# V loads of a decode attention kernel issued by GpSimd instead of SyncE

## The chip, the cores and the metric

The kernel runs on one core of a Trainium2 chip. The time is device microseconds (us) of one execution; the kernel before takes 1980.17 us, the median of 3 runs (1979.96 to 1980.22).

## What is computed

Two attention blocks, A and B, of the same shape are computed one after the other, for a single new token (Sq = 1) against long caches. In each block there are 2 batches, 32 heads with a K and a V cache of 8192 x 192 bf16 each, x of 640 columns, a query weight wq (640 x 6144) and an output weight wo (6144 x 640):

```
q = x @ wq                      # split into 32 heads of 192
scores = q . k_cache * 192**-0.5
p = softmax(scores)             # over the 8192 positions
o = p . v_cache
out = concat_heads(o) @ wo      # A and B side by side in the output
```

Each K and each V of one head and batch is 3.146 MB (8192 x 192 x 2 bytes), and there are 128 of each, so 805 MB of caches are read once, and 31 MB of weights.

## The kernel before, in words

**Units.** The work is cut into NU = 128 units, numbered u: one head of one block for one batch. The two batches of a head follow each other; g = u // 2 counts heads over both blocks. A unit's K and V are laid out on 128 partitions, 64 positions a partition, so that each partition reads one contiguous row of 24,576 bytes from memory (`sp_k`, L198; `sp_v`, L207). K has NK = 2 buffers (`kb`), V has NV = 3 (`vb`).

**One unit.** VectorE multiplies K by the broadcast query, in two halves m0 and m1 (`dve_mul`, L230), into `prod`. TensorE adds `prod` up over groups of 16 columns by matmuls with an identity into PSUM (`pe_sum`, L295: 12 matmuls a half, signals s0 and s1); VectorE reduces what is left to 64 scores a partition (`dve_red`, L233, signals r0, r1), and takes their maximum (`dve_max`, L236). GpSimd makes it one maximum over all partitions (`pool_ar`, L220, signal ar), ScalarE scales it (L243) and takes the exponentials with their sums (`act_exp`, L246, signal exp), GpSimd adds the sums over partitions (`pool_ls`, L224, signal ls). TensorE then multiplies the probabilities with V, 32 matmuls (`pe_pv`, L306, signal pv). Every second unit ScalarE moves the result to SBUF (L253, L254); every fourth it is turned and normalised (f3, L314; f4, L260), and multiplied with wo (f5, L341). The queries of later heads are made by TensorE (L287) ahead of their use, from wq.

**Order on the engines.** Each engine has a list of operations by slot (`dve_tab`, `act_tab`, `pe_tab`, `pool_tab`); slot u is roughly unit u, and inside a slot the operations are sorted by a number. Each engine issues its list in order, and an operation that waits holds up all behind it. On TensorE slot u has the sums of unit u (number 0) and then pv of unit u - 1 (number 2); for the last two units the sums are moved up into slot 125 ahead of pv(124) (L369). On GpSimd slot u has ar(u) (number 0) and ls(u) (number 1).

**Order of the loads.** All cache and weight loads are issued by SyncE (SP), in the order built at L425 to L432 and emitted at L433 to L455: K(0), K(1), V(0), K(2), V(1) and so on, K(u) and then V(u-1), except that K(127) is put right behind K(126), ahead of V(125). K(u) waits for both multiplies of unit u - 2 (its buffer), V(u) for pv(u-3) (its buffer). wq of the next 8 heads and wo of the next 4 heads are put between. K(127) is loaded in two halves, V(126) in 2 parts and V(127) in 4 (VSPLIT, L141), each part with a semaphore of its own; the last two wo tiles follow at the end in a K buffer (L453). ScalarE issues the loads of x and half of the output.

**GpSimd's start.** Ahead of its slots GpSimd builds the identity, clears some tiles, and copies x of block B into its broadcast form (L457 to L467).

Of the kernel before, what the change touches and what calls it, by code (L numbers as in the profile page):

```python
# [51 lines left out]
def build_kernel(nc, blocks, out):  # L52
# [11 lines left out]
    NU = G * B  # L64
# [4 lines left out]
    NV = 3  # L69
# [12 lines left out]
    def unit(u):  # L82
        g = u // B
        return g // Hn, g % Hn, u % B, g
# [7 lines left out]
    with ExitStack() as es:  # L92
# [34 lines left out]
        S_sp = _Stream("sp", sem("s_sp"), reg)  # L127
# [13 lines left out]
        VSPLIT = {NU - 2: [0, T // 2, T], NU - 1: [0, T // 2, 3 * T // 4, 7 * T // 8, T]}  # L141
        vpsem = {(u, i): sem(f"vp{u}_{i}") for u, c in VSPLIT.items() for i in range(len(c) - 1)}

        def key(name, *idx):
            for i in idx:
                if i < 0:
                    return None
            return (name,) + tuple(idx)
# [21 lines left out]
        def dma(out_ap, in_ap, s):  # L170
            return lambda eng: eng.dma_start(out_ap, in_ap).then_inc(s, 16)  # L171
# [4 lines left out]
        def sp_wq(w):  # L176
            blk = (w * HQ) // Hn
            h0 = (w * HQ) % Hn
            src = blocks[blk]["wq"].rearrange("(j c) n -> j c n", c=DC)[:, :, h0 * Dh:(h0 + HQ) * Dh]
            return dma(wqs[:], src, wqsem)  # L180
# [10 lines left out]
        def sp_wo(w):  # L191
            blk = (w * HO) // Hn
            h0 = (w * HO) % Hn
            src = blocks[blk]["wo"][h0 * Dh:(h0 + HO) * Dh, :].rearrange("(pr p i) n -> p pr (i n)", p=128, i=3)
            i = w - (NWO - NLATE)
            return dma(wo_tile(w).rearrange("p pr i n -> p pr (i n)"), src, wosem[w % 2] if i < 0 else wlsem[i])

        def sp_k(u, part=None):  # L198
            blk, h, b, g = unit(u)
            src = blocks[blk]["k"][b, h].rearrange("(p t) d -> p t d", p=128)  # L200
            if part is None:
                return dma(kb[u % NK][:], src, ksem[u % NK])
            if part == 0:
                return dma(kb[u % NK][:, 0:TH, :], src[:, 0:TH, :], ksem[u % NK])
            return dma(kb[u % NK][:, TH:T, :], src[:, TH:T, :], k2sem[u])

        def sp_v(u, t0=0, t1=T, sm=None):  # L207
            blk, h, b, g = unit(u)
            src = blocks[blk]["v"][b, h].rearrange("(p t) d -> p t d", p=128)
            return dma(vb[u % NV][:, t0:t1, :], src[:, t0:t1, :], vsem[u % NV] if sm is None else sm)  # L210

        def vcuts(u):
            c = VSPLIT[u]
            return list(zip(c[:-1], c[1:]))
# [23 lines left out]
        def dve_f2(g):  # L238
            s0 = 64 * (g % 2)
            return lambda eng: eng.reciprocal(rcT[(g // 2) % 2][s0:s0 + 64, :], lall[g % 2][s0:s0 + 64, :])  # L240
# [8 lines left out]
        def act_f1(g, b0, b1):  # L249
            hs = g % 2  # L250

            def fn(eng):
                eng.activation(o_sb[0:1, b0:b1, hs, :], ops[hs][0:1, b0:b1, 0:Dh], ACTF.Identity)  # L253
                return eng.activation(o_sb[32:33, b0:b1, hs, :], ops[hs][32:33, b0:b1, Dh:2 * Dh], ACTF.Identity)  # L254
            return fn
# [22 lines left out]
        def pe_q(qg):  # L278
            pr, b = qg // 2, qg % 2
            g0 = 2 * pr  # L280
            blk = g0 // Hn
            w = g0 // HQ
            off = (g0 % HQ) * Dh

            def fn(eng):
                for c in range(DC):
                    ins = eng.matmul(qps[:, 0:QW], xbc[blk][b][:, c, :], wqs[:, c, off:off + QW],  # L287
                                     start=(c == 0), stop=(c == DC - 1))
                return ins
            return fn, [("wq", w), ("xbc", blk), key("a0", qg - 1)]  # L290
# [61 lines left out]
        pool_tab = [[] for _ in range(NSLOT)]  # L352

        def put(tab, slot, order, fn, waits, sig):
            tab[slot].append((order, len(tab[slot]), fn, waits, sig))

        for u in range(NU):
# [17 lines left out]
            else:  # L375
                cuts = vcuts(u)
                for i, (t0, t1) in enumerate(cuts):
                    put(pe_tab, u + 1, 2, pe_pv(u, t0 // 2, t1 // 2), (w0 if i == 0 else []) + [("vp", u, i)],
                        ("pv", u) if i == len(cuts) - 1 else None)

        for g in range(G):
            u1 = 2 * g + 1
            pp = g // 2
            w1 = [key("f3", pp - 1), ("init",)]
            if g == G - 1:
                put(act_tab, u1, 2, act_f1(g, 0, 1), [("pv", u1 - 1)] + w1, ("f1a", g))
                put(act_tab, u1 + 1, 2, act_f1(g, 1, 2), [("pv", u1), ("f1a", g)], ("f1", g))
            else:
                put(act_tab, u1 + 1, 2, act_f1(g, 0, 2), [("pv", u1)] + w1, ("f1", g))
            put(dve_tab, u1 + 1, 8, dve_f2(g), [("ls", u1), key("f4", pp - 2)], ("f2", g))  # L390
        for pp in range(NP):
# [10 lines left out]
            w = [("f4", pp), ("wo", (2 * pp) // HO), key("f5", pp - 1)]  # L402
# [14 lines left out]
        for qg in range(G):  # L417
            fn, w = pe_q(qg)
# [14 lines left out]
        for kind, u in order:  # L433
            if kind == "k":
                S_sp.add(sp_k(u, 0 if u in k2sem else None), waits=[key("m0", u - NK), key("m1", u - NK)])
                if u in k2sem:
                    S_sp.add(sp_k(u, 1))
                if u == 0:
                    S_sp.add(sp_wq(0))
                w = u // UO  # L440
                if u % UO == 1 and w < NWO - NLATE:
                    S_sp.add(sp_wo(w), waits=[key("f5", ((w - 2) * HO + HO - 1) // 2 if w >= 2 else -1)])
                w = u // UQ
                if u % UQ == UQ - LEAD and w + 1 < NWQ:
                    S_sp.add(sp_wq(w + 1), waits=[key("pq", w * HQ + HQ - 1)])
            else:
                w = [key("pv", u - NV)]
                if u in VSPLIT:
                    for i, (t0, t1) in enumerate(vcuts(u)):
                        S_sp.add(sp_v(u, t0, t1, vpsem[u, i]), waits=w)  # L450
                else:
                    S_sp.add(sp_v(u), waits=w)
        for w in range(NWO - NLATE, NWO):  # L453
            S_sp.add(sp_wo(w), waits=[("m0", NU - 2), ("m1", NU - 2)])
        S_sp.add(out_dma(NBLK - 1, 1), waits=[("oev", NBLK - 1)])  # L455
# [20 lines left out]
        for tab, S in ((dve_tab, S_dve), (act_tab, S_act), (pe_tab, S_pe), (pool_tab, S_pool)):  # L476
            evicted = None
            for slot in range(NSLOT):
                for _, _, fn, waits, sig in sorted(tab[slot], key=lambda e: (e[0], e[1])):
                    if sig is not None and sig[0] in ("pq", "f3", "f3a"):  # L480
                        waits = list(waits) + [evicted]
# [27 lines left out]
def bass_concat_heads__gqa_block_cached__mha_block_cached__decode_kernel(  # L509
    nc: bass.Bass,  # L510
    A_x: bass.AP,
    A_k_cache: bass.AP,
    A_v_cache: bass.AP,
    A_wq: bass.AP,
    A_wo: bass.AP,
    B_x: bass.AP,
    B_k_cache: bass.AP,
    B_v_cache: bass.AP,
    B_wq: bass.AP,
    B_wo: bass.AP,  # L520
    out: bass.AP,
):
    blocks = [
        dict(x=A_x, k=A_k_cache, v=A_v_cache, wq=A_wq, wo=A_wo),
        dict(x=B_x, k=B_k_cache, v=B_v_cache, wq=B_wq, wo=B_wo),
    ]
    build_kernel(nc, blocks, out)
# [28 lines left out]
```

## Time and profile before

| | |
|---|---|
| median of 3 runs | 1980.17 us |
| span of the profiled execution | 1978.0 us |
| TensorE busy (matmuls) | 1651.6 us, 84% |
| VectorE busy | 1056.0 us, 53% |
| GpSimd busy | 121.6 us, 6% |
| bytes moved by DMA | 837.96 MB, mean 424 GB/s |
| DMA queue of SP (q1) | 47,188 packets, 836.78 MB |
| idle of VectorE ahead of its multiplies (L230) | 530.4 us |
| idle of GpSimd ahead of its maxima (L220) | 1710.2 us |

The span runs from the first to the last instruction of the profiled execution; the time of a run is some 2 us more than that span. q1 is the queue of SP's transfers and q10 that of ScalarE's. The page gives an engine's busy time, the DMA rate in 40 slices of the span, the transfers by their issuing line with the median time from issue to landing, and the chain of waits that ended last. PE is TensorE, DVE VectorE, ACT ScalarE, POOL GpSimd; SPq is SP's queue of instructions.

### The profile page before, as it was taken

How to read it: one execution, taken by the hardware profiler on the slowest of the kernel's cores; microseconds unless marked ns; L12 is line 12 of the kernel's file. 1: busy time of each engine (PE TensorE's matmuls, PEld its weight loads, DVE VectorE, ACT ScalarE, POOL GpSimd, SP SyncE). 2: the span in 40 equal slices, each digit the busy share in tenths (PEclk: the TensorE clock that was granted, in tenths of full speed). 3: DMA queues.
4: the chain of work that ended last, by engine and by line, in shares of the span. 5: the costliest groups of instructions: out<-in, count | busy, mean ns of one | idle time of the engine just before them, and what ended most of it. 6: DMA issues, size and time to landing. Idle time of an engine off the chain costs nothing.

```text
span 1978.0 us, 18521 instructions
## 1 busy us (share of the span) xinstructions
PE 1651.6 (84%) x8076; PEld 816.4 (41%) x8076; DVE 1056.0 (53%) x706; ACT 191.3 (10%) x647; POOL 121.6 (6%) x269
## 2 busy tenths in 40 slices
PE   5988888879888888888888878888788977988878
PEld 2444444334444344443444434444344433444434
DVE  4554555545555455655555556555555555556552
ACT  0100101001010010010110101001001000010000
POOL 2200000000000000000000000000000000000001
PEclk9999999999999899998999999998999899998988
DMA  9999999999999999999999999999999999999995
GB/s 402 430 429 430 429 430 431 430 429 430 430 429 429 431 429 430 431 428 430 431 429 430 427 431 431 428 431 427 432 431 427 430 430 430 430 431 429 430 405 236
DMA packets 47856, 837.96 MB, mean 424 GB/s; under 512 B 5144, under 2 KB 5152, under 8 KB 14752
## 3 DMA queue, kind: packets, MB, share of 16 engines
q1 hardware_dynamic: 47188, 836.78, 99.0%
q8 instruction: 63, 1.03, 0.2%
q14 instruction: 17, 0.14, 0.0%
q10 hardware_dynamic: 588, 0.01, 0.0%
HBM read 836.77 MB, written 0.01 MB: 423 GB/s over the span
## 4 chain that ended last, share of the span: by engine, by line
DMA 74%; DVE 11%; issue 10%; PE 4%; POOL 0%; ACT 0%; SPq 0%; DVEq 0%
DMA kb<-in_B_k_cache_dram 38%; DMA kb<-in_A_k_cache_dram 35%; DVE prod L230 11%; PE scps L295 2%; PE ops L306 2%; DMA wqs<-in_A_wq_dram 1%; PE qps L287 0%; PE outps L341 0%; POOL mg L220 0%; PE qps L325 0%; DVE sc L233 0%; ACT qbc L266 0%; ACT pb L246 0%; ACT out_sb L270 0%; SPq L171 0%
## 5 line engine op out<-in xcount | busy, mean ns | idle before, releaser
L230 DVE TENSOR_TENSOR prod<-kb,qbc 128x6144 bf16<-128x6144 bf16 x256 | 848.2, 3355 | 530.4 <-DMA kb<-in_B_k_cache_dram 265.7
L295 PE MATMUL scps<-prod,ident 128*128 128x512 bf16 x3072 | 784.5, 414 | 289.7 <-DVE prod L230 289.4
L306 PE MATMUL ops<-vb,pb 128*33 128x384 bf16 x4096 | 716.4, 335 | 11.4 <-DMA vb<-in_A_v_cache_dram 6.8
L295 PEld LDWEIGHTS scps<-prod,ident 128*128 128x128 bf16 x3072 | 306.0, 105 | 753.7 <-DVE prod L230 370.9
L306 PEld LDWEIGHTS ops<-vb,pb 128*33 128x33 bf16 x4096 | 400.7, 100 | 315.4 <-issue 63.3
L233 DVE TENSOR_REDUCE sc<-scps 128x32 f32<-128x512 f32 x256 | 176.7, 690 | 345.0 <-PE scps L295 344.2
L220 POOL PARTITION_ALL_REDUCE mg<-mp x128 | 63.7, 498 | 1710.2 <-DVE mp L236 1282.2
L243 ACT ACTIVATE nb<-mg 128x1 f32<-128x1 f32 x128 | 26.0, 203 | 1369.1 <-POOL mg L220 1369.1
L287 PE MATMUL qps<-wqs,xbc 128*128 128x384 bf16 x320 | 65.5, 337 | 22.7 <-DMA wqs<-in_A_wq_dram 17.3
L314 PEld LDWEIGHTS qps<-ones,o_sb 33*128 33x128 f32 x372 | 67.1, 257 | 13.1 <-issue 13.1
L314 PE MATMUL qps<-ones,o_sb 33*128 33x1 f32 x372 | 69.7, 311 | 0.0
L224 POOL PARTITION_ALL_REDUCE lall<-rs x128 | 53.2, 416 | 116.9 <-ACT pb L246 116.9
L253 ACT ACTIVATE o_sb<-ops 1x384 f32<-1x384 f32 (+1 forms) x65 | 30.8, 475 | 248.6 <-PE ops L306 248.6
L246 ACT ACTIVATE pb<-sc,nb 128x64 bf16<-128x64 f32 x128 | 52.3, 408 | 14.0 <-PE ops L306 9.8
L287 PEld LDWEIGHTS qps<-wqs,xbc 128*128 128x128 bf16 x320 | 26.7, 99 | 56.5 <-issue 20.5
L266 ACT ACTIVATE qbc<-qps 128x384 bf16<-128x384 f32 x64 | 31.4, 490 | 141.7 <-PE qps L287 141.0
L254 ACT ACTIVATE o_sb<-ops 1x384 f32<-1x384 f32 (+1 forms) x65 | 31.0, 476 | 0.8
L236 DVE TENSOR_REDUCE mp<-sc 128x1 f32<-128x64 f32 x128 | 28.2, 220 | 4.4
L341 PE MATMUL outps<-wos,oTz 128*4 128x320 bf16 x168 | 27.4, 299 | 0.0
L246 ACT ACTIVATION_READ_ACCUMULATOR pb<-sc,nb 128x1 f32 x128 | 23.8, 186 | 0.0
L341 PEld LDWEIGHTS outps<-wos,oTz 128*4 128x4 bf16 x168 | 11.9, 84 | 17.6 <-issue 11.9
L240 DVE RECIPROCAL rcT<-lall 64x2 f32<-64x2 f32 x64 | 9.9, 154 | 12.7 <-POOL lall L224 11.7
(21 smaller groups left out, 33.2 us busy)
## 6 DMA issues: line engine op xcount, KB each, us to landing
kb<-in_A_k_cache_dram SPq DMA_DIRECT2D x64, 3072.0 KB, 22.5
vb<-in_A_v_cache_dram SPq DMA_DIRECT2D x64, 3072.0 KB, 29.5
kb<-in_B_k_cache_dram SPq DMA_DIRECT2D x63, 3072.0 KB, 22.5
vb<-in_B_v_cache_dram SPq DMA_DIRECT2D x62, 3072.0 KB, 29.8
wqs<-in_A_wq_dram SPq DMA_DIRECT2D x4, 1920.0 KB, 29.0
wos<-in_A_wo_dram SPq DMA_DIRECT2D x8, 960.0 KB, 24.4
wqs<-in_B_wq_dram SPq DMA_DIRECT2D x4, 1920.0 KB, 29.0
wos<-in_B_wo_dram SPq DMA_DIRECT2D x6, 960.0 KB, 24.4
```

Of the source, the lines that this page charges most:

```text
L220: return lambda eng: eng.partition_all_reduce(mg[u % 2][:], mp[u % 2][:], 128, bass.bass_isa.ReduceOp.max)
L224: return lambda eng: eng.partition_all_reduce(lall[g % 2][:, b:b + 1], rs[u % 2][:], 128, bass.bass_isa.ReduceOp.add)
L230: return lambda eng: eng.tensor_tensor(prod[hf][:], kb[u % NK][:, hf * TH:(hf + 1) * TH, :], q, ALU.mult)
L233: return lambda eng: eng.tensor_reduce(sc[u % 2][:, hf * TH:(hf + 1) * TH], scps[hf][:], AXL.X, ALU.add)
L246: return lambda eng: eng.activation(pb[u % 2][:, :, ::32], sc[u % 2][:].rearrange("p (j a) -> p j a", a=2), ACTF.Exp, bias=nb[u % 2][:], s ...
L254: return eng.activation(o_sb[32:33, b0:b1, hs, :], ops[hs][32:33, b0:b1, Dh:2 * Dh], ACTF.Identity)
L266: return lambda eng: eng.activation(qbc[qg % NQ][:], qps[:, 0:QW].rearrange("p (a d) -> p a d", a=2), ACTF.Identity)
L287: ins = eng.matmul(qps[:, 0:QW], xbc[blk][b][:, c, :], wqs[:, c, off:off + QW], start=(c == 0), stop=(c == DC - 1))
L295: ins = eng.matmul(scps[hf][:], ident[:], prod[hf][:, :, j * DG:(j + 1) * DG], start=(j == 0), stop=(j == NJ - 1))
L306: ins = eng.matmul(ops[(u // B) % 2][0:33, b, 0:QW], pb[u % 2][:, j, :], vv[:, j, :], start=(j == 0), stop=(j == TH - 1))
L314: ins = eng.matmul(oTps[:, 2 * i + b:2 * i + b + 1], o_sb[:, b, :, :].rearrange("p s (r i) -> p i (s r)", i=3)[:, i, :], ones33[:], start= ...
L341: ins = eng.matmul(outps[0:4, 0:NH2], oTz[:, pp % NZ, i, 2 - 2 * half:6 - 2 * half], wt[:, pr, i, half * NH2:(half + 1) * NH2], start=(fir ...
```

## The change

The V loads of units 0 to 125 (all but the split ones) are taken out of SP's list and put in GpSimd's: V(0) and V(1) at the head of slot 0, ahead of ar(0), and V(u) at the head of slot u - 1, ahead of ar(u-1) and ls(u-1), with the same wait for pv(u-3), the same rows and the same semaphore as before. GpSimd's transfers go to a queue of their own, whose descriptors are written by software on GpSimd. K, wq, wo, and the parts of V(126) and V(127) stay on SP in their old order.

```
+        for u in range(NU):
+            if u not in VSPLIT:
+                put(pool_tab, max(u - 1, 0), -2 if u else -3, sp_v(u), [key("pv", u - NV)], None)
...
                 if u in VSPLIT:
                     for i, (t0, t1) in enumerate(vcuts(u)):
                         S_sp.add(sp_v(u, t0, t1, vpsem[u, i]), waits=w)
-                else:
-                    S_sp.add(sp_v(u), waits=w)
```

## The prediction

> **What bounds the kernel now.** I read the profile page first: its slices, the queues, the DMA issues. DMA runs at 429 to 431 GB/s in nearly every slice, and only the last two fall off; nearly all bytes are on one queue.
>
> ```profile
> DMA  9999999999999999999999999999999999999995
> GB/s 402 430 429 430 429 430 431 430 429 430 430 429 429 431 429 430 431 428 430 431 429 430 427 431 431 428 431 427 432 431 427 430 430 430 430 431 429 430 405 236
> ...
> q1 hardware_dynamic: 47188, 836.78, 99.0%
> ...
> kb<-in_A_k_cache_dram SPq DMA_DIRECT2D x64, 3072.0 KB, 22.5
> vb<-in_A_v_cache_dram SPq DMA_DIRECT2D x64, 3072.0 KB, 29.5
> ```
>
> One K or V transfer is 128 x 24,576 bytes = 3.146 MB, so at 430 GB/s it takes **7.3 us**, and a unit (one K, one V) 14.6 us. Next, the waits: the multiply waits for K, and hardly anything waits for V (columns: total us, times, longest).
>
> ```profile
> DVE prod L230 <- DMA kb<-in_B_k_cache_dram: 265.7, 63, 9.5
> DVE prod L230 <- DMA kb<-in_A_k_cache_dram: 259.4, 60, 9.4
> ...
> PE ops L306 <- DMA vb<-in_A_v_cache_dram: 6.8, 4, 2.4
> ```
>
> So the kernel runs as fast as bytes come, until the last K has been waited for. From there the end is set by compute. The chain of waits (columns: start, length, what), near its end, and the timeline of VectorE there:
>
> ```profile
> 1903.40 22.52 DMA kb<-in_B_k_cache_dram
> ...
> 1940.43 7.99 PE scps L295 x24
> 1948.41 15.71 PE ops L306 x96
> ```
> ```profile
> 1896.75 6.63 DVE L230 TENSOR_TENSOR prod<-kb,qbc 128x6144 bf16<-128x6144 bf16 x2 [4.18 <-DMA kb<-in_B_k_cache_dram]
> ...
> 1911.37 6.63 DVE L230 TENSOR_TENSOR prod<-kb,qbc 128x6144 bf16<-128x6144 bf16 x2 [2.99 <-DMA kb<-in_B_k_cache_dram]
> ...
> 1925.95 6.63 DVE L230 TENSOR_TENSOR prod<-kb,qbc 128x6144 bf16<-128x6144 bf16 x2 [3.13 <-DMA kb<-in_B_k_cache_dram]
> ...
> 1937.04 6.60 DVE L230 TENSOR_TENSOR prod<-kb,qbc 128x6144 bf16<-128x6144 bf16 x2
> ```
>
> These are units 124 to 127. Units 125 and 126 begin when their K lands, 14.6 us apart; unit 127 begins 11.1 us after 126 without waiting for its K, which is the compute pace (two multiplies, the sums on TensorE, two reductions, the maximum). From unit 126's start to the end of the span are 1978.0 - 1925.95 = **52.05 us of compute**, in which the DMA engines are only 60% busy (the window's row). What decides the time is thus when K of units 125 and 126 land, that is, **how many V transfers have been served ahead of them**.
>
> **The change, part by part.**
>
> *Order of service.* SP's queue is first in, first out: K(u-1), V(u-2), K(u). When K(u) lands, u-1 V transfers (0 to u-2) are done: 124 when K(125) lands. After, V has a queue of its own. How does a DMA engine share two filled queues? The one stretch of the trace that shows it is the start, where ScalarE's queue (x, packets of 10 bytes) runs against SP's (rows of 24,576 bytes). From 4 to 10 us:
>
> ```profile
> q1 hardware_dynamic: 97, 2.29, 93.5%
> q10 hardware_dynamic: 97, 0.00, 0.9%
> ```
>
> 97 packets against 97: turn by turn, one packet each, whatever the size. K and V rows are both 24,576 bytes (the whole run's count of packets of 8 KB and more is 47,856 - 14,752 = 33,104, about 128 for each K and V), so if the software queue also makes one packet of a row, each gets half. A wq or wo load on SP's queue has small packets (3,072 and 3,840 bytes): beside it V gets nearly all.
>
> So V runs ahead as far as its three buffers let it. V(u) waits for pv(u-3); in the trace pv(122) ends at 1896.9, 0.1 us after unit 124 starts, so V(125) is issued at about the start of unit 124, two units before its old place (1918.87). It follows V(124), issued a unit earlier, without a gap. Say it starts 2 us into unit 124; in the remaining 12.6 us, at half rate, 12.6 / 14.6 = 0.86 of it is served. So 125.86 V transfers are done when K(125) lands, not 124: 1.86 x 7.3 = **13.6 us later** (1925.0). K(126) then needs the rest of V(125) and its own 7.3 us, about 8.3 us, less than the compute pace; so unit 126 starts 11.1 us behind unit 125, not 14.6, and **3.5 us come back**. Sum: 13.6 - 3.5 = **+10.1 us**.
>
> If descriptors are written only after the multiplies that run then (6.6 us into the unit), 0.55 of V(125) is served: 1.55 x 7.3 = 11.3, less 3.5: **+7.8**. The floor, as long as V(125) ends ahead of K(126), is one transfer, +7.3. I take **+9**, between them.
>
> *Issue on POOL.* The trace has no DMA issued by POOL. The nearest rows below: SP's issue of a V load, 0.43 us. The nearest above: a POOL instruction beside VectorE's multiply, 6.71 us where it mostly takes 0.35:
>
> ```profile
> 56.50 6.71 POOL L220 PARTITION_ALL_REDUCE mg<-mp  x1 [3.91 <-DVE rcT L240]
> ```
>
> It ended with the multiplies of 56.39 to 62.99. Either way the cover holds: queued behind V(u) on POOL is ar(u-1), which can't start before the maximum, 11 us into the unit; V(u)'s wait is met by 0 to 5 us (later where wq's and wo's products run), so even a 6.7 us issue ends about then. Its result is needed by pv(u-1) 10 us into the next unit, another 14 us of cover. POOL's idle time before L220 is 1710.2 us, 13 a unit. Cost 0; were that cover gone, ScalarE's exponentials and then TensorE's pv would be late. For the two ends of the range this term is the one from +10.1 to +7.8. The Trainium skill, SBUF — State Buffer, "Who interferes with whom", holds that a tensor_tensor takes only the read side of the port pair that VectorE and GpSimd share, and so doesn't hold up descriptor writing; by it the +10.1 end holds, while the 6.71 us row is of an instruction that reads.
>
> *Issue on SP.* SP loses 126 issues of 0.43 us, which lie behind 1766 us of its waiting for multiplies: nothing. No K waits on SP for a V in this trace (its one wait for TensorE, 33.4 us, is the split V of unit 127, which stays).
>
> *Start.* POOL reaches V(0) after its memsets and xbc copies, at 17.2 us; V(0) and V(1) go out then. wq landed at 17.3, so unit 0 (19.76) isn't delayed. SP's queue holds K(0), wq, K(1), wo(0) = 9.2 MB, to about 23 us: no gap. K(2) and K(3) share with V and land about where compute wants them (45.7 and 56.4): nothing of its own; what V takes there is counted above.
>
> *End.* V(126) and V(127) stay on SP, V(127) still waits for pv(124), which TensorE runs after the sums of unit 127: the 52.05 us follow K(126) unchanged. Nothing.
>
> **Sum.** Profiled span 1978.0 + 9 = 1987.0. The median of the runs is 1980.17, 2.2 us over that span, so **1989.2 us** (1987.5 to 1990.3 for +7.3 to +10.1), 0.5% slower. Bytes and packets stay as they are. About 0.2% (4 us) is what a measurement of this kernel can tell from no change.
>
> **Rivals.**
>
> *The second queue costs transfer time* (slower still). Against: packets of SP's queue keep the engines full now (100.3% of 16 engines over 100 to 1900 us). For: in the shared stretch 97 pairs took 6 us of 16 engines, 0.99 us a pair, against 0.912 + 0.009 for the packets themselves; 0.07 us lost. That stretch is a cold start (first packets took up to 1.9 us), so it is an upper end: 126 x 8 = 1008 V packets per engine x 0.07 = +70 us, the lower end 0. Also, the slowest engine paces: in the trace the 16 counts of a K arrive over 1.5 us for unit 0 but over 12.7 us for unit 120. An engine that lost another 10 to 20 ns on each V packet would cost 10 to 20 us on top: **2000 to 2010**, to 2060 at the row's end. The Trainium skill, DMA: Bandwidth & Descriptors, "Latency and other measured facts", says that engines 7 and 15 are usually slower, with the software queue's descriptor ring as a guess at the cause; nothing in this trace shows that. Chance 0.18.
>
> *K gets ahead* (the other side: not slower). If the software queue's packets are shorter than K's rows, turn-taking gives K most of the rate. Then V is late: K(u) is held only by its two buffers, and multiplies by TensorE, which waits in order at pv(u-3). K(126) lands with 124 V served, not 125: one transfer earlier, -7.3, and V(124) and V(125) still arrive within the 22 us before TensorE wants them: **1972.9**. The point from which it decides: V(125) not yet served when K(126) lands. For: V hardly ever releases anything now, so it has room. Against: rows as whole packets. Chance 0.15.
>
> *Two queues hide the gap between packets.* Packets of 3,072 bytes took 121 ns, of 24,576 bytes 912 ns: 36.8 ns per KB (of 1000 bytes) and 8 ns per packet. About 2,060 rows per engine x 8 ns = 16.5 us at most; with +9, **1972.7**. Against: one packet at a time is all the trace shows. Chance 0.05.
>
> *It doesn't matter, or doesn't do what it says*: the software queue's packets come in the old order (V starts so late that it ends where it ended), or the loss and a half of the gap cancel: 1977 to 1984, about **1980**. The Trainium skill, DMA: Bandwidth & Descriptors, "Rules for kernel authors", says that spreading DMAs over issuing engines doesn't help bandwidth; that rate the forecast keeps too, and order alone moves. Chance 0.07.
>
> **The numbers.** Forecast 0.55. Slower 0.55 + 0.18 = 0.73, same 0.07, faster 0.15 + 0.05 = 0.20. The range goes from 1972 (K ahead, or the gap hidden) to 2014 (forecast plus 25 ns a V packet); outside are the larger queue costs and a little below, under 2 in 10.
>
> **What would show it.** V loads on a second queue with 16,128 packets of 24,576 bytes; rate still 430 GB/s up to about 1900; K's time to landing still about 22.5 us, V's about 15, not 29.5; units 125 and 126 starting near 1925 and 1936, 11 us apart instead of 14.6; 52 us from there to the end; SP's 33.4 us wait unchanged. The forecast is wrong if V's packets are smaller or their queue slower (V waits at L306, K early), if the mid-run rate moves by more than 1 GB/s (4.5 us), or if POOL's reductions start late.

## The result, and the profile after

The changed kernel takes **1991.53 us** (median of 4 runs, 1990.59 to 1995.03) against 1980.20 us before (4 runs, 1979.96 to 1980.36): a ratio of 1.0061, 95% interval 1.0047 to 1.0075. The forecast was 1989.2 us. The profiled execution, the fastest of the four, has a span of 1988.8 us, 10.8 us more than before.

The page of the changed kernel: the rates of the 40 slices, then the queues (packets, MB, share of 16 engines), then issues by line with the median us from issue to landing.

```profile
GB/s 404 428 431 430 428 430 427 430 431 429 430 430 428 430 429 430 420 429 430 426 430 423 430 430 429 430 417 430 427 431 430 414 430 418 429 431 428 432 426 188
...
q1 hardware_dynamic: 29044, 440.41, 52.0%
q0 software_dynamic: 18144, 396.37, 46.6%
...
kb<-in_A_k_cache_dram SPq DMA_DIRECT2D x64, 3072.0 KB, 22.5
vb<-in_A_v_cache_dram POOLq DMA_DIRECT2D x64, 3072.0 KB, 20.0
kb<-in_B_k_cache_dram SPq DMA_DIRECT2D x63, 3072.0 KB, 22.5
vb<-in_B_v_cache_dram POOLq DMA_DIRECT2D x62, 3072.0 KB, 23.8
wqs<-in_A_wq_dram SPq DMA_DIRECT2D x4, 1920.0 KB, 41.1
```

The change did what it says: q0 holds 126 x 128 = 16,128 rows and 126 x 16 completion counts, together 18,144. A row is still one packet. K still takes 22.5 us from issue to landing. The rate is at 427 to 432 GB/s in most slices, with single slices down to 414. The waits of the two kernels differ little: VectorE's multiplies still wait for K (its reductions wait 359 us for TensorE's sums, 344 before), and no wait for V is left.

```profile
DVE prod L230 <- DMA kb<-in_A_k_cache_dram: 260.9, 57, 16.2
DVE prod L230 <- DMA kb<-in_B_k_cache_dram: 260.6, 55, 15.9
```

The longest single wait for K is now 16.2 us; it was 9.5. The timeline of VectorE at the end (start, length; in brackets the idle time ahead), units 124 to 127:

```profile
1907.64 6.63 DVE L230 TENSOR_TENSOR prod<-kb,qbc 128x6144 bf16<-128x6144 bf16 x2 [4.19 <-DMA kb<-in_B_k_cache_dram]
...
1922.26 6.63 DVE L230 TENSOR_TENSOR prod<-kb,qbc 128x6144 bf16<-128x6144 bf16 x2 [2.98 <-DMA kb<-in_B_k_cache_dram]
...
1936.87 6.63 DVE L230 TENSOR_TENSOR prod<-kb,qbc 128x6144 bf16<-128x6144 bf16 x2 [3.18 <-DMA kb<-in_B_k_cache_dram]
...
1947.90 6.60 DVE L230 TENSOR_TENSOR prod<-kb,qbc 128x6144 bf16<-128x6144 bf16 x2
```

Unit 126 starts at 1936.87, 10.9 us later than before, and from there to the end it is 1988.8 - 1936.87 = 51.9 us (before 52.05). So **the whole loss is there when K(126) lands**, and nothing is added after it.

When does it arise? For each unit I took the start of its first multiply less that of the same unit before (*delay*), and from the completion counts in the trace the number of V transfers that had landed by then, with the part of the next one by the time between its landing and the last, less the u - 1 of the old order (*lead*). What the lead does not explain is delay - 7.3 x lead (the *rest*). The changed kernel:

| unit | delay, us | lead, V transfers | rest, us |
|---|---|---|---|
| 1 | 0.1 | - | - |
| 6 | 10.1 | 1.38 | 0.1 |
| 18 (weights) | 15.1 | 2.15 | -0.6 |
| 25 | 8.5 | 1.12 | 0.4 |
| 58 (weights) | 18.0 | 2.56 | -0.7 |
| 65 | 7.5 | 0.98 | 0.4 |
| 95 | 8.1 | 0.92 | 1.4 |
| 105 | 12.7 | 1.31 | 3.1 |
| 125 | 10.9 | 0.98 | 3.7 |

The loss is there from unit 3 on, follows the lead up and down, and a rest of some 4 us comes up late in the run. The rest is known only roughly: with the rows of V that had been served by then, in place of landings, the lead at unit 125 is 1.04 and the rest 3.3 us. A unit without weights takes 14.6 us in both kernels. So most of the loss is no price per transfer that adds up: it is a debt that stays, V transfers that were served ahead of K.

### The profile page after: what moved, and what is told of

Same layout as the page of the kernel before. It is cut to its first block, busy times and chain, and to the rows that moved or that the text cites. A ratio compares the mean times of both kernels' runs of the same rounds, so it can differ in the third digit from the quotient of the medians.

```text
span 1988.8 us, 18521 instructions
## 1 busy us (share of the span) xinstructions
PE 1637.2 (82%) x8076; PEld 816.0 (41%) x8076; DVE 1056.4 (53%) x706; ACT 191.6 (10%) x647; POOL 269.4 (14%) x395
## 4 chain that ended last, share of the span: by engine, by line
DMA 71%; DVE 12%; issue 9%; PE 7%; ACT 0%; SPq 0%; DVEq 0%
DMA kb<-in_B_k_cache_dram 36%; DMA kb<-in_A_k_cache_dram 34%; DVE prod L230 12%; PE scps L295 4%; PE ops L306 3%; DMA wqs<-in_A_wq_dram 1%; PE outps L341 0%; PE qps L287 0%; DVE sc L233 0%; PE qps L325 0%; PE qps L314 0%; ACT qbc L266 0%; ACT o_sb L254 0%; ACT o_sb L253 0%; ACT out_sb L270 0%
## 5 line engine op out<-in xcount | busy, mean ns | idle before, releaser
L306 PE MATMUL ops<-vb,pb 128*33 128x384 bf16 x4096 | 708.0, 333 | 0.0
L220 POOL PARTITION_ALL_REDUCE mg<-mp x128 | 80.2, 626 | 1161.9 <-DVE mp L236 800.9
L224 POOL PARTITION_ALL_REDUCE lall<-rs x128 | 113.8, 889 | 116.9 <-ACT pb L246 116.9
L287 PE MATMUL qps<-wqs,xbc 128*128 128x384 bf16 x320 | 65.5, 337 | 22.3 <-DMA wqs<-in_A_wq_dram 16.9
L171 POOL DMA_DIRECT2D vb<-in_A_v_cache_dram x64 | 36.8, 575 | 201.6 <-PE ops L306 201.4
L171 POOL DMA_DIRECT2D vb<-in_B_v_cache_dram x62 | 35.3, 569 | 210.1 <-PE ops L306 204.3
L287 PEld LDWEIGHTS qps<-wqs,xbc 128*128 128x128 bf16 x320 | 26.7, 99 | 56.0 <-issue 17.7
L246 ACT ACTIVATION_READ_ACCUMULATOR pb<-sc,nb 128x1 f32 x128 | 23.8, 186 | 0.0
## 6 DMA issues: line engine op xcount, KB each, us to landing
kb<-in_A_k_cache_dram SPq DMA_DIRECT2D x64, 3072.0 KB, 22.5
kb<-in_B_k_cache_dram SPq DMA_DIRECT2D x63, 3072.0 KB, 22.5
vb<-in_B_v_cache_dram POOLq DMA_DIRECT2D x62, 3072.0 KB, 23.8
wqs<-in_A_wq_dram SPq DMA_DIRECT2D x4, 1920.0 KB, 41.1
```

Source lines behind the costliest of these rows:

```text
L220: return lambda eng: eng.partition_all_reduce(mg[u % 2][:], mp[u % 2][:], 128, bass.bass_isa.ReduceOp.max)
L224: return lambda eng: eng.partition_all_reduce(lall[g % 2][:, b:b + 1], rs[u % 2][:], 128, bass.bass_isa.ReduceOp.add)
L246: return lambda eng: eng.activation(pb[u % 2][:, :, ::32], sc[u % 2][:].rearrange("p (j a) -> p j a", a=2), ACTF.Exp, bias=nb[u % 2][:], s ...
L306: ins = eng.matmul(ops[(u // B) % 2][0:33, b, 0:QW], pb[u % 2][:, j, :], vv[:, j, :], start=(j == 0), stop=(j == TH - 1))
```

## The experiments

The theory: with two filled queues the engines take turns, V is served ahead of its old place, and each V transfer ahead of a K delays it by 7.3 us; a little more is lost around weight loads; which kind of queue it is doesn't matter. The first rival: the software queue costs time for each transfer. The times below are compared with runs of the kernel before on the same chip (1979.66 us for experiments 1 to 4, 1979.90 us for 5 to 8). Delays and leads are those of one profiled execution each.

**1. The same queues, but hardware.** V goes to ScalarE's queue, at the same place in its list.

```
-  put(pool_tab, max(u - 1, 0), -2 if u else -3, sp_v(u), [key("pv", u - NV)], None)
+  put(act_tab, max(u - 1, 0), -2 if u > 1 else -0.5, sp_v(u), [key("pv", u - NV)], None)
```

> Order theory (a second queue lets V be served ahead of K, 7.3 us of delay for each V transfer, and some 4 us are lost around weight loads): the V loads on ScalarE's hardware queue share the engines just as well, so the time stays at 1987 to 1995 us and the last K's land some 10 us later than before. Rival (the software queue itself costs transfer time or issue time): without it the time falls back to 1980 to 1984 us.

Measured: 1988.42 us, ratio 1.0047 (1.0030 to 1.0063). Its page:

```profile
q1 hardware_dynamic: 29044, 440.41, 52.0%
q10 hardware_dynamic: 18732, 396.38, 46.7%
```

Without any software queue nearly all of the loss is there, with the same course: delay 10.2 us at unit 6, 9.0 at 15, 16.2 at 18, 10.5 at 125. What the software queue as such can carry is, by the medians, the 3 us between the two kernels, of whose runs the nearest are 1.2 us apart. A price of any second queue, of either kind, is not excluded by this run; that takes experiment 2.

**2. The last V loads back.** V(118) to V(125) return to SP's queue in the old order, on semaphores of their own.

```
-            if u not in VSPLIT:
+            if u < 118:
                 put(pool_tab, ...)
...
+                elif u >= 118:
+                    S_sp.add(sp_v(u, 0, T, vtsem[u % NV]), waits=w)
```

> V loads of units 0 to 117 on GpSimd, those of 118 to 127 back on SyncE in the old order. Order theory: the lead of V is worked off by the end, K of unit 126 lands with 125 V transfers done as before, and only what is lost around weight loads stays: 1980 to 1985 us. Rival (each transfer of the software queue costs): 118 of 126 transfers still pay, so 1989 to 1991 us.

Measured: 1982.54 us, ratio 1.0021 (1.0008 to 1.0033). The delay is 7.3 to 17.9 us from unit 3 to 117, 8.7 at 118, 4.5 at 119, 1.5 at 120 and 1.5 at 126. VectorE, units 126 and 127:

```profile
1927.40 6.63 DVE L235 TENSOR_TENSOR prod<-kb,qbc 128x6144 bf16<-128x6144 bf16 x2 [4.92 <-DMA kb<-in_B_k_cache_dram]
...
1939.24 6.60 DVE L235 TENSOR_TENSOR prod<-kb,qbc 128x6144 bf16<-128x6144 bf16 x2
```

118 transfers went over the software queue, and the debt was given back within two units once V stood behind K again. A price per transfer could not be given back, so the rival falls in its main form. Two things limit this. The 10 runs spread from 1979.98 to 1992.02 us, and the trace is of one at 1980.63. And up to unit 117 this kernel gives the engines the same work as the changed one and as the one of experiment 6, yet the rests at unit 117 are 0.9 us here, 4.5 in the changed kernel and 4.9 in experiment 6: the rest differs from execution to execution.

**3. K instead of V on GpSimd.** K(2) to K(127) go to GpSimd's list with their old waits (slot u - 2), all else stays on SP.

```
+            put(pool_tab, u - NK, -2, sp_k(u, 0 if u in k2sem else None),
+                [key("m0", u - NK), key("m1", u - NK)], None)
```

> K loads of units 2 to 127 on GpSimd, V and the weights on SyncE. Order theory: now K has a queue of its own, weights hold up V and not K, K lands earlier than before by up to one transfer: 1973 to 1981 us. Rival (the software queue costs): 126 K transfers pay, 1989 us or more.

Measured: 1984.89 us, ratio 1.0027 (1.0017 to 1.0036): a miss for both. The lead explains it, and shows what I forgot: on SP the V loads had stood behind K's waits. Without K in that queue V waits for its buffers alone, and runs ahead. At unit 125 the lead is 0.50, the delay 3.5 us, and 7.3 x 0.50 = 3.7. In the middle the delay goes to 0 and to -5.0 (unit 90) where weights in V's queue hold V up.

**4. Weights in V's queue.** As the changed kernel, but wq 1 to 7 and wo 1 to 13 are issued by GpSimd too (slot u - 2, on semaphores apart from those of the first ones).

```
-                    S_sp.add(sp_wq(w + 1), waits=[key("pq", w * HQ + HQ - 1)])
+                    put(pool_tab, u - 2, -1, sp_wq(w + 1), [key("pq", w * HQ + HQ - 1)], None)
```

> As the changed kernel, but the weight loads wq 1 to 7 and wo 1 to 13 too go out on GpSimd, in V's queue. Order theory: small weight packets then take their turns at V's cost and not at K's, the jumps of K at weight loads go, and so do the some 4 us lost there; V still ends ahead of the last K: 1984 to 1989 us. Rival (the software queue costs): more of its packets, 1991 to 1993 us.

Measured: 1985.54 us, ratio 1.0029 (1.0018 to 1.0040). Its page has more on the software queue than that of the changed kernel, and it is faster:

```profile
q0 software_dynamic: 22368, 422.91, 49.9%
q1 hardware_dynamic: 20916, 413.87, 48.8%
```

At weight loads K now gains (delay -8.7 us at unit 59, -7.8 at 107) where it lost 14 to 19 us; the jumps do not go, a unit later the delay is 9.1 and 9.4. At unit 125 the lead is 0.78, the delay 5.2, the rest -0.5. That fits a rest that belongs to weights standing in another queue than V, and not to the software queue, but it does not show it alone: the rest also differs between executions (experiment 2), and this edit changed the weights' packets too. They are 6,144 and 7,680 bytes long in q0, 3,072 and 3,840 on SP's queue, for the same loads. Where a rest arises is seen in the changed kernel's DMA rates after a weight load, 1500 to 1560 us (40 slices of 1.5 us; busy share in tenths, GB/s):

```profile
DMA  8999989999999999999999999999597997997998
GB/s 360 462 425 405 492 379 457 457 411 442 442 393 442 426 426 442 393 475 442 393 459 459 393 442 442 393 442 410 213 262 295 459 459 344 508 459 344 492 448 360
```

From 1542 to 1546.5 the rate is half to two thirds of the usual one: V had been served while K waited, its buffers are full, and K(101) has to wait for unit 99, which started late. By the packets of the trace V's queue is empty from 1535.4 to 1543.9, and K(101), issued at 1544.3, has its first row only at 1548.2, 3.3 us after K(100) landed. Some engines have nothing to do for a while; the rest rises from 0.9 us at unit 100 to 3.3 at 101.

**5. V held to K's pace.** V(u), from u = 1, waits for the second multiply of its own unit as well, and stands in slot u.

```
+  put(pool_tab, u, -2, sp_v(u), [key("pv", u - NV), ("m1", u) if u else None], None)
```

> As the changed kernel, but V(u) (from u = 1) waits for the second multiply of its own unit too, not only for its buffer, so it goes out one unit later and 6.6 us into the unit. Order theory: when K(u) lands about 0.5 V transfers less or more than half a transfer are served ahead of the old order, lead 0.3 to 0.6, delay 2 to 5 us, no jumps to 15 us at weight loads: 1981 to 1986 us. Rival (the software queue costs per transfer, whenever it is issued): 1989 us or more.

Measured: 1984.58 us, ratio 1.0025 (1.0016 to 1.0034). Less V ahead, less loss; but my figure for the lead was wrong. It is about 0 away from weight loads (-0.01 at unit 125) and up to 0.87 right behind them, and the 4.4 us of delay at unit 125 are rest, 1.0 at unit 15 and 4.5 at 125. I put that down to the weights, still in K's queue; no run shows it apart.

**6. One V load back.** Only V(125) returns to SP, behind K(127).

```
-            if u not in VSPLIT:
+            if u < NU - 3:
...
+                elif u == NU - 3:
+                    S_sp.add(sp_v(u, 0, T, v125sem), waits=w)
```

> Only V(125) goes back to SyncE, behind K(127) as before. Order theory: K(126) no longer shares with V(125), unit 126 starts at the compute pace, 11.1 us behind unit 125 instead of 14.6: 3.5 us less than the changed kernel, 1987 to 1989 us. Rival (queue cost per transfer): 1 of 126 transfers, no difference, 1990 to 1992 us.

Measured: 1987.53 us, ratio 1.0036 (1.0022 to 1.0049). VectorE, units 125 to 127:

```profile
1923.10 6.63 DVE L233 TENSOR_TENSOR prod<-kb,qbc 128x6144 bf16<-128x6144 bf16 x2 [3.08 <-DMA kb<-in_B_k_cache_dram]
...
1934.46 6.62 DVE L233 TENSOR_TENSOR prod<-kb,qbc 128x6144 bf16<-128x6144 bf16 x2
...
1945.88 6.60 DVE L233 TENSOR_TENSOR prod<-kb,qbc 128x6144 bf16<-128x6144 bf16 x2
```

Unit 126 follows 125 by 11.4 us without waiting for its K; in the changed kernel by 14.6 with a wait. One transfer of 126 moved, and 3.2 us come back in the trace (delay 11.7 us at unit 125, 8.5 at 126), near the 3.5 expected; the medians are 4.0 us apart.

**7. Half rows.** Each V load is two, of half a row each, so that V's packets are half as long as K's.

```
+  put(pool_tab, max(u - 1, 0), -2 if u else -3, sp_v(u, 0, TH), [key("pv", u - NV)], None)
+  put(pool_tab, max(u - 1, 0), -2 if u else -3, sp_v(u, TH, T), [], None)
```

> Each V load on GpSimd as two loads of half a row (packets of 12,288 bytes), 8 ns more per row by the durations of the packets, about 8 us over the run. If queues take turns by packet, V now gets a third and K two thirds while both are filled: K runs ahead, units start at most 5 us later than before by mid-run, TensorE waits for V at pv, and the time is 1978 to 1986 us. If they share by bytes, K is as late as in the changed kernel and the packets cost 8 us on top: 1996 to 2001 us.

Measured: 1991.92 us, ratio 1.0060 (1.0046 to 1.0074): neither. The kind of behaviour is that of turns by packet, though the delay is no small one throughout: it swings between -2.4 and 18.3 us. K is ahead at the start (delay -2.4 us at unit 4, where the changed kernel has 9.8), and TensorE now waits for V:

```profile
PE ops L306 <- DMA vb<-in_B_v_cache_dram: 124.6, 25, 9.6
PE ops L306 <- DMA vb<-in_A_v_cache_dram: 118.8, 26, 9.6
```

What I mis-sized is the price of the packets. From 100 to 1800 us two halves took 2 x 464.2 = 928.4 ns, a row before 915.9, and K's rows 917.1: 12.5 + 1.2 = 13.7 ns, times about 1000 rows of each in an engine, is 13.7 us, not 8. The delay at unit 127 is 12.4 us. That the gain of K's being ahead is lost in this price fits the numbers; no run separates the two.

**8. The other sign.** The kernel before, one queue, no load of GpSimd. From unit 114 on the second half of V(u) goes behind K(u + 2) instead of behind K(u + 1).

```
 before:  K(117) V(116)             K(118) V(117)             ...
 now:     K(117) V(115)b V(116)a    K(118) V(116)b V(117)a    ...
```

> The kernel before, all on SyncE's queue; from unit 114 on the second half of V(u) goes behind K(u + 2) instead of K(u + 1). Order theory, other sign: K of the last units lands half a transfer (3.6 us) earlier, the end follows: 1976 to 1978 us. Rival (the order of K and V does not matter, only the queue): 1979.5 to 1980.5 us.

Measured: **1977.06 us**, ratio 0.9985 (0.9976 to 0.9994). Units 126 and 127:

```profile
1923.63 6.63 DVE L231 TENSOR_TENSOR prod<-kb,qbc 128x6144 bf16<-128x6144 bf16 x2 [1.92 <-DMA kb<-in_B_k_cache_dram]
...
1935.70 6.60 DVE L231 TENSOR_TENSOR prod<-kb,qbc 128x6144 bf16<-128x6144 bf16 x2
```

The delay is 0.3 us up to unit 115, -3.3 at 116 and -2.3 at 126, and the span is 2.5 us less than before. K earlier by 2.3 us, the end earlier by 2.5: within one queue the order moves the time, here to the other side, though the edit also halves the rows of these V loads. It is the one version that beats both kernels, by 0.15%.

## Why the prediction was right, and where it was not

*Bound by bytes until K(126), then 52 us of compute.* Right: 51.9 us after, and the loss is complete when unit 126 starts (delay 10.9 us; the span grew by 10.8).

*Turns of one packet each.* Right for this kernel: V rows are whole packets, K keeps 22.5 us to its landing, and with half rows V falls behind (run 7). Following the changed kernel's packets from end to start between 1905 and 1921 us, some four in five stretches of K or of V on an engine are one row long. The Trainium skill, DMA: Bandwidth & Descriptors, "Queues, rings and completion order", says that each DMA engine goes round the queues packet by packet, with typically 9 to 17 descriptors in a packet; the runs agree on the turns, and in them a turn is one row. The weight loads, whose packets are short, are put back most: wq of block A takes 41.1 us to land, and 29.0 in the kernel before:

```profile
wqs<-in_A_wq_dram SPq DMA_DIRECT2D x4, 1920.0 KB, 29.0
```

*V(125) 0.86 served when K(125) lands, +13.6 us.* **Wrong in size.** V(125) was issued when I said (1908.08, 0.4 us into unit 124), but it did not follow an emptying queue: V(124) was still ahead of it and landed at 1922.5, together with K(125). I had taken V to be as far ahead as its buffers allow at all times. It is so only just behind weight loads (lead 2.0 to 2.6); in the units between, both queues are filled, each gets half, and the lead stays where the last weight load left it, mostly 0.9 to 1.4. So the term is 0.98 x 7.3 = 7.2 us. The sign to look for was V's time to landing: I expected 15 us, and it is 20.0 and 23.8. For V(125) it is 29.5, twice the 14.6 us of one V load at half rate: two V loads in the queue and not one.

*3.5 us come back at unit 126.* **Did not occur**: V(125) still shared the engines with K(126), and unit 126 came 14.6 us behind unit 125. With V(125) out of the way it does occur (run 6), so the step failed with the one before it.

*Weight loads in the middle of the run: no term in the sum.* **That left out some 4 us**: the rest at unit 125 is 3.7 us, and behind a weight load both queues can run dry for a moment (run 4). One of the forecast's own signs of being wrong came with it: from 100 to 1900 us the rate fell from 430 to 428 GB/s, and 1 GB/s was the limit named. So 7.2 + 3.7 = 10.9 us; forecast were 13.6 - 3.5 = 10.1, and 9 was taken. The debt was put 6.4 us too high; the 3.5 us that did not come back and the 3.7 us left out made up for it. That the sum came out near is luck; the mechanism and the sign were right, the terms were not.

*Issue on POOL: nothing.* Right, and cheaper than I bounded it. The issue of V(125), in the middle of VectorE's multiplies of 1907.64 to 1914.27:

```profile
1908.08 0.57 POOL L171 DMA_DIRECT2D vb<-in_B_v_cache_dram  x1 [2.99 <-PE ops L306]
...
1948.00 6.71 POOL L220 PARTITION_ALL_REDUCE mg<-mp  x1 [12.68 <-DVE rcT L240]
```

0.57 us for the issue, while the maximum over partitions beside the multiplies of unit 127 took 6.71 us. Nor did the writing of descriptors wait for VectorE: V(100), issued at 1542.62 into an empty queue during the multiplies of 1537.65 to 1544.28, has its first row at 1543.90. The Trainium skill, SBUF — State Buffer, "Who interferes with whom", has it so, the part on descriptors as an inference: a tensor_tensor keeps GpSimd from reading, not from writing descriptors. GpSimd's reductions did get longer (L224 889 ns on the mean, 416 before); the 51.9 us at the end show nothing of it.

*The rival of a costly queue.* Rejected as the main cause by runs 1 and 2; run 4, with more on the software queue and less time, agrees. A small price of a second queue of either kind may be there: from 100 to 1800 us V's rows took 918.7 ns on the mean in q0, and as much in ScalarE's queue, against 915.9 for the rows before; 2.8 ns x 1000 is some 3 us at most, and in the traced execution of run 2, with 118 of the transfers, all but 1.5 us of delay were gone at unit 126. I did not test it apart from the rest at weight loads. Open too is why the rest differs between executions of the same work (run 2), and with it whether it is really smaller with ScalarE's queue (1.4 us at unit 125) than with GpSimd's (3.7).

## What to carry to other kernels

Where one filled queue feeds the engines, as here, its order is a schedule: it says which transfer is late and which early. In these runs a second filled queue replaced that order by turns of a packet each, so a transfer with room to spare pushed back the one that everything waits for, while the rate stayed nearly the same (428 GB/s against 430). Ask of such a change what stands ahead of the critical load after it, count that in transfers, and read from the time to landing of the other loads how many of them are in flight. At the end of a kernel that is bound by bytes, put first what the last chain of compute needs; run 8 gained 0.15% by it.

## What the runs showed of the hardware beside that

- The 16 counts of one K do not arrive together: in the kernel before the first comes 2.1 us ahead of the last at unit 4, 7.1 at unit 60 and 13.2 at unit 125, as if some engines were 0.7% quicker. In the changed kernel it is 4.7 us at unit 125. Of the lower mean rate of the middle (428 GB/s against 430 over 1800 us, some 8 us) only a part shows as a loss: from unit 6 to unit 125 the delay grew by 0.8 us, and the rest by 3.6. A kernel whose first engines run far ahead of the last has moved bytes that nobody waits for yet, which may be the other part; no run shows it.
- The small packets of a weight load take turns with rows of 24,576 bytes: K(58), behind such a load in SP's queue, landed 26.7 us after K(57); in the kernel before, with the same load ahead of it, 16.9.
- The spread of the times is wider with two filled queues: 1990.59 to 1995.03 us in 4 runs, and 1979.98 to 1992.02 in the 10 runs of the second experiment, against 1979.96 to 1980.36 before.
- The same weight loads had packets twice as long in GpSimd's software queue (6,144 and 7,680 bytes, run 4) as in SP's (3,072 and 3,840). The rows of K and V were one packet of 24,576 bytes in every queue.
